# Divisors of the attention rows: inverted in a compact form by way of memory

## The chip, the core and the metric

The kernel runs on one core of a Trainium2 chip. A core has a matrix engine (TensorE: PE in the profile, its weight loads PEld), a vector engine (VectorE, DVE), an engine for activation functions (ScalarE, ACT), a general one (GpSimd, POOL) and one that here only issues transfers (SyncE, SP). Each works through its own instructions in order and waits on semaphores for the others; 16 DMA engines move data between memory (HBM) and the on-chip memory (SBUF). Matmuls write their results into PSUM. The metric is the device time in microseconds. Before the change its median is 1020.46 us over 6 runs (1018.83 to 1021.18).

## The reference

Attention among tokens of one cluster, and then a feed-forward block on the result. q, k and v are 4 x 8 x 768 x 64, with 16 centroids per head:

```python
q_assign = np.argmax(np.einsum('bhsd,hcd->bhsc', q_n, c_n), axis=-1)
k_assign = np.argmax(np.einsum('bhsd,hcd->bhsc', k_n, c_n), axis=-1)
mask = q_assign[:, :, :, None] == k_assign[:, :, None, :]
scores = scale * np.matmul(q, k.transpose(0, 1, 3, 2))
scores = np.where(mask, scores, -1000000000.0)
scores = scores - np.max(scores, axis=-1, keepdims=True)
attn = np.exp(scores)
attn = attn / (np.sum(attn, axis=-1, keepdims=True) + 1e-09)
attn_out = np.matmul(attn, v)
# (B,H,S,D) -> x of (B*S, H*D) = 3072 x 512
h = x @ w_in                    # 512 x 2048
out = (h - np.tanh(h)) @ w_out  # 2048 x 512
```

The weights arrive as 64-bit floats and are turned into 32-bit ones on the chip. What the change touches is the division by `np.sum(attn)`: one number for each query and head.

## The kernel before

Two heads make a pair: 4 batches of 4 pairs, 16 pairs `n`. The 64 feature rows of the first head lie on partitions 0 to 63 and those of the second on 64 to 127. The 768 queries of a pair are worked in two halves of 384, and the 768 keys of a half in three steps of 256: 96 steps in all. In batch 0 the first halves of its four pairs come first and then the second halves; in later batches both halves of a pair follow each other.

A step, in the loop from line 943 on, does this. `begin` (L410) makes the scores of the next step on TensorE and their exponentials on ACT. `select` (L442) masks them on VectorE by comparing the cluster code of each query (`row`, the codes of all queries on every partition, read from memory by a broadcast, L376) with that of the key; POOL adds the masked tiles up (L459, L463). `value` (L465) multiplies them with v. In the first halves of batch 0 (`summed`) the sums are made on TensorE instead (L481), and for pairs 1 to 3 the mask is added to the scores by a matmul with one-hot codes (`hot`, L385 to L398, L429). After the third step of a half `take` (L488) copies the result to `xT`, and `total` (L493) sums the exponentials over the partitions with a matmul against ones. Since that matmul has 64 equal columns per head, its result `den` (128 x 384) holds on each of the 64 partitions of a head the same 384 sums. ACT copies it with the 1e-9 added (L504), and POOL adds it into `wholes` (L505). In the next step `divide` (L507) is called three times: it inverts 128 of the 384 columns each time on VectorE (L510), and the last call multiplies `xT` by the inverse (L513) and has POOL add the inverse into `inverses` (L514). At the end `wholes` and `inverses` are compared with bounds (L1029); they decide with other tests whether a general path must run, which it doesn't for these inputs.

The feed-forward block of a batch is worked beside the attention of the next one, as a list of small items (`plain_items` for batch 0, `strassen_items` with seven products in place of eight for the others); the share of a step in this list is fixed by `fills`. Results wait in PSUM tiles of the pool `ps_f`, which has three. `todo` holds the other work of a step (maskings, routing, the divisions, weight pieces, combining of factors, repeated reads of the inputs) and is spread between the items by `between` (L1007). So the order on each engine is written out by the program, and nothing is moved at run time. In the first 19 steps, two per step at most, the weights arrive in 32 pieces: a POOL transfer of 512 KB (`fetch`, L192; three buffers), one ACT instruction (L139) and three on VectorE (L144, L148, L151). The transfer for the third piece ahead is issued once L148 has freed the buffer.

SP issues in order: loads of q, k and v (L289), the codes out to memory and back (`publish` L369, `spread` L376, `spread_both` L385), the combined weight factors out (L590, L609) and back as `stream` tiles of about 1 MB, asked two ahead (L648), and repeated reads of inputs (L869, L871). At each wait all that stands behind it waits too.

Of the kernel before, what the change touches and what calls it, by code (L numbers as in the profile page):

```python
# [30 lines left out]
F32 = mybir.dt.float32  # L31
# [3 lines left out]
ALU = mybir.AluOpType  # L35
# [3 lines left out]
P = 128  # L39
# [9 lines left out]
MOST_INVERSE = 2.0**5  # L49
SUM_MOST = 2.0**80  # L50
# [7 lines left out]
def kernel(  # L58
# [10 lines left out]
    nc = tc.nc  # L69
# [3 lines left out]
    B, H, S, D = q.shape  # L73
# [4 lines left out]
    HP = H // 2  # L78
# [3 lines left out]
    TB = S // 2  # L82
    HCH = NCH // 2
# [8 lines left out]
    const = ctx.enter_context(tc.tile_pool(name="const", bufs=1))  # L92
    dram = ctx.enter_context(tc.tile_pool(name="dram", bufs=6, space=DRAM))
# [6 lines left out]
    inverses = const.tile([P, TB], F32, name="inverses")  # L100
    wholes = const.tile([P, TB], F32, name="wholes")
    smallest = const.tile([P, 2 * len_pieces], F32, name="smallest")
    largest = const.tile([P, 4 * (HP - 1)], F32, name="largest")
    flag = const.tile([1, 1], I32, name="flag")

    out_r = out.rearrange("(b p j) m -> b j p m", p=P, j=NCH)
# [46 lines left out]
    def fast():  # L153
# [121 lines left out]
        pairs = [(b, p) for b in range(B) for p in range(HP)]  # L275
# [73 lines left out]
        def summed(n: int, half: int):  # L349

            return n < HP and half == 0
# [50 lines left out]
        xT, scores, weights, sums, avs = {}, {}, {}, {}, {}  # L402
# [83 lines left out]
        dens = {}  # L486

        def take(n: int, half: int):  # L488
            if half == 0:
                xT[n] = xp.tile([P, 2, TB], F32, name="xT")  # L490
            nc.scalar.copy(out=xT[n][:, half], in_=avs.pop((n, half)))

        def total(n: int, half: int):  # L493

            s = sums.pop((n, half))
            ps = s
            if not summed(n, half):
                ps = ps_f.tile([P, TB], F32, name="den", tag="f")
                for h in range(2):
                    nc.tensor.matmul(  # L500
                        ps[h * D : h * D + D], lhsT=ones, rhs=s[:, h], start=True, stop=True
                    )
            t = dens[n, half] = sump.tile([P, TB], F32, name="den")
            nc.scalar.activation(out=t, in_=ps, func=ACT.Copy, bias=EPS)  # L504
            nc.gpsimd.tensor_tensor(out=wholes, in0=wholes, in1=t, op=ALU.add)  # L505

        def divide(n: int, half: int, part: int):  # L507
            c = slice(part * P, (part + 1) * P)
            t = dens[n, half]
            nc.vector.reciprocal(out=t[:, c], in_=t[:, c])  # L510
            if part == HCH - 1:
                x = xT[n][:, half]
                nc.vector.tensor_tensor(out=x, in0=x, in1=t, op=ALU.mult)  # L513
                nc.gpsimd.tensor_tensor(out=inverses, in0=inverses, in1=dens.pop((n, half)), op=ALU.add)  # L514
# [68 lines left out]
        def up_maker(q: int):  # L583

            lo, hi = w_in[q], w_in[q + NQ4 // 2]
            a11, a12, a21, a22 = lo[:, 0:CH], lo[:, CH:CD], hi[:, 0:CH], hi[:, CH:CD]

            def keep(which, t):
                for c in range(CH):
                    nc.sync.dma_start(  # L590
                        up_factors[
                            q * FQ : (q + 1) * FQ, :, c, SLOT[which]
                        ].rearrange("i p f -> p i f"),
                        t[:, c].rearrange("p (i f) -> p i f", f=P),
                    )

            return maker(
                (a11, a12, a22), (1, 2, 4),
                ((5, a21, a22, ALU.add), (7, a11, a21, ALU.subtract), (6, 5, a11, ALU.subtract),
                 (3, a12, 6, ALU.subtract)),  # L600
                keep, [P, CH, FQ * P],
            )
# [253 lines left out]
        for n in range(1, HP):  # L856
            b, p = pairs[n]
# [80 lines left out]


        paces = {3: 1, 4: 1}  # L940
        late, divides, makers = [], [], []
        fill, whole, spent, since, over = [], 0.0, 0.0, 0, 1
        for at, (n, half, s) in enumerate(steps):
            b, p = pairs[n]
# [9 lines left out]
            if at == 2 * HALF:  # L954
                makers = [it for i in range(2) for it in up_maker(i)]
# [17 lines left out]
            value(n, half, s)  # L973
            if s == NS - 1:
                take(n, half)
                divides = [lambda n=n, half=half, i=i: divide(n, half, i) for i in range(HCH)]

                if p == HP - 1 and (half == 1 or b == 0):
                    total(n, half)
                    late += divides  # L980
                    divides = []
                if half == 1:
                    load(n + (HP if n < 2 else 2), (2,) if n < 2 or n >= HP else ())

            todo = []
            if following:
                todo += [lambda i=i: select(*following[:2], 2 * following[2] + i) for i in range(2)]
            todo += [stages[i] for i in (5, 3, 4, 2) if i in stages]
            todo += late
            late = []  # L990
            if divides:
                todo.append(lambda n=n, half=half: total(n, half))
                late, divides = divides, []
# [34 lines left out]
        for t, bound in ((inverses, MOST_INVERSE), (wholes, SUM_MOST), (largest, LARGE)):  # L1028
            nc.vector.tensor_scalar(out=t, in0=t, scalar1=bound, scalar2=None, op0=ALU.is_le)  # L1029
        nc.vector.tensor_tensor(out=wholes, in0=wholes, in1=inverses, op=ALU.mult)  # L1030
        checks = [largest]
        if words == 2:
            nc.vector.tensor_scalar(
                out=smallest, in0=smallest, scalar1=HIGH_LEAST, scalar2=None, op0=ALU.is_ge
# [198 lines left out]
```

## Time and profile before

| | us |
|---|---|
| median of 6 runs | 1020.46 |
| profiled execution, its own time | 1023.01 |
| span of that execution, first to last instruction | 1021.2 |
| PE busy | 992.6 (97%) |
| VectorE busy | 613.5 (60%) |
| POOL busy | 552.5 (54%) |
| ACT busy | 298.4 (29%) |
| reciprocals L510, 96 of 128 x 128 | 83.3 |
| POOL adds L505 and L514, 32 each | 35.2 and 41.8 |

In the profile an instruction has its line, engine, operation, the tile written and those read, and its shape as partitions x elements. "Idle before" is the time in which its engine stood idle just before it, with the instruction or transfer that ended most of that. The stages in time are: up to 105 us the first halves of batch 0, to 230 us its second halves, to 403 us batch 1, to 640 us batch 2 and to 866 us batch 3; then only the feed-forward block of batch 3 is left. A transfer issued by SP shows the time of its issue, not of its landing; the landing is read from whoever waits for it, or from the DMA engines' share.

### The profile page before, as it was taken

To read this page: it belongs to the slowest core of one execution; us is meant where nothing else is said; L and a number is where in the kernel's file an instruction comes from. 1 tells how busy PE (TensorE), PEld (TensorE's weight loads), DVE (VectorE), ACT (ScalarE), POOL (GpSimd) and SP (SyncE) were. 2 spreads that over 40 slices of the span, in tenths; PEclk is the share of its full clock that TensorE was granted. 3 is DMA by queue.
4 is the path that set the end of the run, shared out by engine and by line. 5 is a ranking of instruction groups with operands and counts; after the bars stand their busy time and mean duration, and the time that the engine had idled before them with its cause. 6 is when DMAs were issued, how large, how long until landed. Compare 5 with 4: busy or idle time off the path is not lost.

```text
span 1021.2 us, 16368 instructions
## 1 busy us (share of the span) xinstructions
PE 992.6 (97%) x6444; PEld 471.5 (46%) x6444; DVE 613.5 (60%) x1088; ACT 298.4 (29%) x458; POOL 552.5 (54%) x387
## 2 busy tenths in 40 slices
PE   8988899999999999999999999999999999999997
PEld 4433343334444333444455555444445555444664
DVE  6588788336976856676756456766765545543011
ACT  4444334123433233323332222333332211122000
POOL 1124353445655655677789345576879545466600
PEclk9999999999999999999999999999999999999999
DMA  8653423022826633335444555444332322333221
GB/s 214 167 173 127 147 83 116 11 57 74 218 59 178 230 111 100 118 127 173 146 144 140 158 168 152 149 153 138 118 132 91 103 94 66 111 109 121 103 95 38
DMA packets 105736, 127.92 MB, mean 125 GB/s; under 512 B 55604, under 2 KB 85428, under 8 KB 102964
## 3 DMA queue, kind: packets, MB, share of 16 engines
q1 hardware_dynamic: 99268, 105.26, 33.2%
q0 software_dynamic: 6240, 21.50, 6.1%
q8 instruction: 53, 0.87, 0.4%
q14 instruction: 31, 0.25, 0.1%
q10 hardware_dynamic: 144, 0.03, 0.0%
HBM read 105.74 MB, written 21.03 MB: 124 GB/s over the span
## 4 chain that ended last, share of the span: by engine, by line
PE 90%; DVE 4%; ACT 1%; POOL 1%; DMA 1%; issue 1%; ACTq 0%; DVEq 0%; POOLq 0%
PE pu L722 21%; PE pd L770 20%; PE sc L418 13%; PE av L472 13%; PE o L548 8%; PE h L532 7%; PE sim L318 2%; PE den L500 2%; PE pt L299 2%; DMA raw<-in_moe_w_out_dram 1%; PE den L481 1%; PE warm L269 1%; DVE den L510 1%; PE pr L331 1%; ACT t L306 1%
## 5 line engine op out<-in xcount | busy, mean ns | idle before, releaser
L463 POOL TENSOR_TENSOR sum<-sum,e 128x768 f32<-128x768 f32 x112 | 208.6, 1863 | 78.0 <-DVE e L450 74.0
L450 DVE SCALAR_TENSOR_TENSOR e<-row,code,sc 128x384 f32<-128x384 bf16 x336 | 185.9, 607 | 81.6 <-ACT sc L440 70.0
L770 PE MATMUL pd<-stream,G 128*64 128x256 f32 x1728 | 192.4, 380 | 2.4 <-POOL G L713 2.4
L440 ACT ACTIVATE sc<-sc 128x768 f32<-128x768 f32 x168 | 126.0, 793 | 212.1 <-PE sc L418 187.9
L418 PE MATMUL sc<-t,t 64*128 64x384 f32 x768 | 151.7, 513 | 4.8 <-ACT rest L139 2.9
L770 PEld LDWEIGHTS pd<-stream,G 128*64 128x64 f32 x1728 | 123.3, 137 | 70.8 <-issue 8.0
L472 PE MATMUL av<-e,vals 128*64 128x384 f32 x768 | 146.8, 501 | 1.4 <-DVE e L450 0.9
L713 POOL TENSOR_TENSOR G<-G,th 128x768 f32<-128x768 f32 x48 | 86.8, 1820 | 88.7 <-ACT th L712 88.7
L722 PE MATMUL pu<-xT,stream 128*64 128x384 f32 x768 | 134.5, 487 | 0.0
L722 PE MATMUL pu<-diff,stream 128*64 128x384 f32 x576 | 103.5, 488 | 1.0 <-DVE u L708 0.6
L418 PEld LDWEIGHTS sc<-t,t 64*128 64x128 f32 x768 | 66.4, 187 | 79.6 <-issue 39.2
L532 PE MATMUL h<-xT,w_in 128*64 128x384 f32 x512 | 88.9, 498 | 3.8 <-DVE g L539 3.1
L510 DVE RECIPROCAL den<-den 128x128 f32<-128x128 f32 x96 | 83.3, 911 | 11.9 <-POOL wholes L505 11.9
L472 PEld LDWEIGHTS av<-e,vals 128*64 128x64 f32 x768 | 47.1, 136 | 86.9 <-issue 82.6
L548 PE MATMUL o<-w_out,g 128*64 128x512 f32 x384 | 85.9, 593 | 0.0
L722 PEld LDWEIGHTS pu<-xT,stream 128*64 128x64 f32 x768 | 54.6, 137 | 67.3 <-issue 61.8
L459 POOL TENSOR_TENSOR sum<-e 128x768 f32<-128x768 f32 x28 | 56.7, 2025 | 49.3 <-DVE e L450 49.3
L712 ACT ACTIVATE th<-G 128x768 f32<-128x768 f32 x48 | 40.3, 844 | 114.8 <-DVE G L708 114.8
L722 PEld LDWEIGHTS pu<-diff,stream 128*64 128x64 f32 x576 | 40.5, 137 | 51.6 <-issue 44.2
L505 POOL TENSOR_TENSOR wholes<-wholes,den 128x384 f32<-128x384 f32 x32 | 35.2, 1100 | 51.3 <-ACT den L504 51.3
L532 PEld LDWEIGHTS h<-xT,w_in 128*64 128x64 f32 x512 | 37.1, 140 | 51.4 <-issue 45.4
L514 POOL TENSOR_TENSOR inverses<-inverses,den 128x384 f32<-128x384 f32 x32 | 41.8, 1305 | 34.2 <-DVE den L510 34.0
(116 smaller groups left out, 888.6 us busy)
## 6 DMA issues: line engine op xcount, KB each, us to landing
stream<-up_factors SPq DMA_DIRECT2D x24, 896.0 KB
stream<-down_factors SPq DMA_DIRECT2D x21, 1024.0 KB
raw<-in_moe_w_in_dram POOLq DMA_DIRECT2D x16, 512.0 KB, 4.5
raw<-in_moe_w_out_dram POOLq DMA_DIRECT2D x16, 512.0 KB, 4.3
again<-in_moe_w_in_dram SPq DMA_DIRECT2D x32, 256.0 KB
again<-in_moe_w_out_dram SPq DMA_DIRECT2D x32, 256.0 KB
x<-in_q_dram SPq DMA_DIRECT2D x32, 192.0 KB
x<-in_k_dram SPq DMA_DIRECT2D x32, 192.0 KB
```

What stands on the lines that cost most here:

```text
L418: nc.tensor.matmul(sc[i][:, h, 0:TB], lhsT=turned[n, 1][r].rearrange("p a n -> p (a n)")[:, j * P : (j + 1) * P], rhs=turned[n, 0][r, half ...
L440: nc.scalar.activation(out=out, in_=sc[i][:, :, 0:TB], func=ACT.Exp, scale=SCALE)
L450: nc.vector.scalar_tensor_tensor(out=e[:, h], in0=rows[n, half][:, h], scalar=codes[n][:, 1, j // HCH, h, j % HCH : j % HCH + 1], in1=sc[: ...
L459: nc.gpsimd.tensor_tensor(out=s, in0=pair[0], in1=pair[1], op=ALU.add)
L463: nc.gpsimd.tensor_tensor(out=s, in0=s, in1=pair[i], op=ALU.add)
L472: nc.tensor.matmul(avs[n, half][h * D : h * D + D], lhsT=vals[n][:, h, j], rhs=e[i][:, h], start=(j == 0), stop=(j == NCH - 1),)
L510: nc.vector.reciprocal(out=t[:, c], in_=t[:, c])
L532: nc.tensor.matmul(h[r], lhsT=w_in[i][:, c, o * P : (o + 1) * P][:, r], rhs=xT[c][:, half], start=(c == 0), stop=(c == CD - 1),)
L548: nc.tensor.matmul(acc[sub][r], lhsT=gs[f % HF][:, f // HF, sub * P : (sub + 1) * P][:, r], rhs=w_out[f // FQ][:, f % FQ], start=(f == seq ...
L713: nc.gpsimd.tensor_tensor(out=g[:, f].rearrange("p a n -> p (a n)"), in0=g[:, f].rearrange("p a n -> p (a n)"), in1=th.rearrange("p a n -> ...
L722: nc.tensor.matmul(ps[r], lhsT=streams[base + i][:, c, k_, r], rhs=right[c], start=(c == 0), stop=(c == CH - 1),)
L770: nc.tensor.matmul(ps[r], lhsT=left(i)[:, r], rhs=t[:, i], start=(i == 0), stop=(i == HF - 1))
```

## The change

For the first three pairs of each batch (24 of the 32 halves) the sums are no longer inverted on 128 partitions. `last(n)` names the fourth pair, which keeps the old way. For the others four stages are called in four successive steps, the first in the step in which `total` stood before:

- `total`: as before up to the copy L504; then, in place of the POOL add, two SP transfers write one row of 384 sums of each head to memory (`list`).
- `compact`: an SP transfer reads the 768 sums back as 128 partitions x 6 into a place of its own in the new tile `each`.
- `invert`: VectorE inverts the 128 x 6; an SP transfer writes them to memory (`back`), and two more read each head's row of 384 onto its 64 partitions of `den`.
- `scale`: VectorE multiplies `xT` by `den`.

The POOL adds into `wholes` and `inverses` remain for the fourth pairs alone. At the end three VectorE instructions of 128 x 144 compare `each` with the bounds.

```diff
+    each = const.tile([P, 2 * B * (HP - 1), 2 * TB // P], F32, name="each")
...
             nc.scalar.activation(out=t, in_=ps, func=ACT.Copy, bias=EPS)
-            nc.gpsimd.tensor_tensor(out=wholes, in0=wholes, in1=t, op=ALU.add)
+            if last(n):
+                nc.gpsimd.tensor_tensor(out=wholes, in0=wholes, in1=t, op=ALU.add)
+                return
+            lists[n, half] = dram.tile([2, TB], F32, name="list")
+            for h in range(2):
+                nc.sync.dma_start(lists[n, half][h : h + 1], t[h * D : h * D + 1])
+        lists, spots = {}, {}
+        def last(n: int):
+            return pairs[n][1] == HP - 1
+        def compact(n: int, half: int):
+            spots[n, half] = each[:, len(spots)]
+            nc.sync.dma_start(
+                spots[n, half], lists.pop((n, half)).rearrange("h n -> (h n)").rearrange("(p i) -> p i", p=P)
+            )
+        def invert(n: int, half: int):
+            t = spots[n, half]
+            nc.vector.reciprocal(out=t, in_=t)
+            back = dram.tile([2, TB], F32, name="back")
+            nc.sync.dma_start(back.rearrange("h n -> (h n)").rearrange("(p i) -> p i", p=P), t)
+            for h in range(2):
+                nc.sync.dma_start(
+                    dens[n, half][h * D : h * D + D], back[h : h + 1].to_broadcast([D, TB])
+                )
+        def scale(n: int, half: int):
+            x = xT[n][:, half]
+            nc.vector.tensor_tensor(out=x, in0=x, in1=dens.pop((n, half)), op=ALU.mult)
...
-        late, divides, makers = [], [], []
+        late, divides, makers, later = [], [], [], {}
...
-                divides = [lambda n=n, half=half, i=i: divide(n, half, i) for i in range(HCH)]
+                if last(n):
+                    divides = [lambda n=n, half=half, i=i: divide(n, half, i) for i in range(HCH)]
+                else:
+                    for i, stage in enumerate((total, compact, invert, scale)):
+                        later.setdefault(at + i, []).append(
+                            lambda stage=stage, n=n, half=half: stage(n, half)
+                        )
...
-            todo += late
+            todo += late + later.pop(at, [])
...
-        checks = [largest]
+        inverse = each.rearrange("p a b -> p (a b)")
+        fits = inverses[:, 0 : inverse.shape[1]]
+        nc.vector.tensor_scalar(
+            out=fits, in0=inverse, scalar1=MOST_INVERSE, scalar2=None, op0=ALU.is_le
+        )
+        nc.vector.scalar_tensor_tensor(
+            out=fits, in0=inverse, scalar=1.0 / SUM_MOST, in1=fits, op0=ALU.is_ge, op1=ALU.mult
+        )
+        checks = [fits, largest]
```

## The prediction, made before the changed kernel was run

> **What bounds the kernel now.** I read the page first, then the busy time by stage, then TensorE's own waits, then the chain of waits and the order of time where TensorE waits.
>
> The page and the busy time by stage (columns: length, then PE, PEld, DVE, ACT, POOL busy with instruction counts, granted clock, DMA share, GB/s):
> ```profile
> span 1021.2 us, 16368 instructions
> PE 992.6 (97%) x6444; PEld 471.5 (46%) x6444; DVE 613.5 (60%) x1088; ACT 298.4 (29%) x458; POOL 552.5 (54%) x387
> L510 DVE RECIPROCAL den<-den 128x128 f32<-128x128 f32 x96 | 83.3, 911 | 11.9 <-POOL wholes L505 11.9
> ...
> 60.00:130.00 70.00, 58.63 (x322) 23.67 (x318) 58.04 (x89) 28.31 (x47) 27.96 (x29) 0.92 0.48 156
> 130.00:405.00 275.00, 273.37 (x1502) 109.72 (x1500) 188.88 (x282) 93.88 (x147) 145.94 (x92) 1.00 0.37 111
> 405.00:875.00 470.00, 467.15 (x3246) 233.28 (x3242) 291.39 (x546) 131.59 (x198) 310.83 (x211) 1.00 0.41 133
> ```
> TensorE is the bound, and a full one: from 130 to 875 us it idles 1.63 + 2.85 = 4.5 us of 745. VectorE's 83.3 us of reciprocals are mostly beside it. Only in 60 to 130 us does TensorE idle (11.4 us), and there VectorE is busy 58 of 70 us. TensorE's waits in that stage, in 130 to 865 us, and the chain:
> ```profile
> PE h L532 <- DVE g L539: 3.1, 1, 3.1
> PE sc L418 <- ACT rest L139: 2.9, 1, 2.9
> PE sc L429 <- DVE hot L397: 2.5, 1, 2.5
> ...
> PE sim L318 <- ACT t L306: 1.2, 5, 0.2
> PE pd L770 <- POOL G L713: 0.9, 2, 0.5
> ...
> 61.46 2.50 DVE den L510 x3
> 78.76 2.59 DVE den L510 x3
> 86.25 4.37 DMA raw<-in_moe_w_out_dram
> 95.62 2.59 DVE den L510 x3
> ```
> The chain runs through three sets of reciprocals. Those at 61.46 (pair 1) and 78.76 (pair 2) go away; the one at 95.62 is pair 3, the last of its batch, and stays. The 2.5 us wait at 67.3 to 69.8 us is for the one-hot rows that stand on VectorE behind the first set. The 2.9 us wait, 88.6 to 91.5, ends with the masking at 90.23, which follows weight pieces behind the second set.
>
> **What goes.** 24 of the 32 halves lose three reciprocals (72 x 0.911 = 65.6 us of VectorE), the POOL add into `wholes` (1.0 to 1.1) and that into `inverses` (1.3): 24 x 2.4 = 58 us of POOL. The x multiply (0.56) stays, two steps later. From 130 us on the cover is TensorE's own work, so 21 of the halves are worth nothing by themselves. Pair 0's set (40.6 to 43.2 us) lies where TensorE is 97 to 100% busy: nothing either.
>
> **What comes.** Per half six SP transfers in place of none: two rows out (list), one spread in (compact), one out (back), two broadcasts; 144 in all. VectorE gets one 128x6 reciprocal. No row has that shape: the 128x1 one takes 0.16 us, a 128x128 one 0.91; by count I take 0.16 + 0.04 = 0.2. ACT and PE keep their instructions. List and compact have a step or more and nobody waits for them. Back and broadcast have one step: VectorE inverts at step +2 and multiplies at +3, in order, so a late broadcast holds maskings, evictions and weight pieces behind it. SP stands at three waits per half (sum copied, list landed, back landed), and behind it queue code rows, stream loads and repeated weight reads. Code rows have a step to spare. Streams are asked two ahead, each for 9 us of matmuls (7 products of 1.29 us): the 2 to 6 us that SP stands are covered; without that, each us is a us of TensorE.
>
> **The two hops.** Nearest rows:
> ```profile
> 39.54 0.32 SPq L369 DMA_DIRECT2D q_codes<-qc  x1
> ...
> 40.87 1.27 SPq L385 DMA_DIRECT2D hot<-q_codes  x2
> ...
> 46.94 0.42 DVE L393 TENSOR_SCALAR hot<-hot,mine_code 128x768 bf16<-128x768 bf16 x1 [0.44 <-DMA hot<-q_codes]
> ```
> A small write to DRAM lets SP go on 40.87 - 39.54 = 1.33 us after its issue (2.69 at 57.10, with weight loads about). The broadcast: code rows of 192 KB, as much as ours, issued at 204.46, kept the DMA engines busy to 207.1, 2.6 us. The hot broadcast, twice our bytes with loads behind it, took 6.1 us. So the chain from reciprocal to usable divisor is 1.3 + 2.6 + 0.1 = 4.0 us at best, and 2.7 + 6.1 = 8.8 us loaded at worst; I take 4.6 to 5.4 in the weight stage, nearer the rows of our size. The steps there are 4.6 us of TensorE, in batch 1 some 7.2 us (24 steps in 229 to 402.7), later 9.7 (46 in 402.7 to 847).
>
> (The Trainium skill, "DMA: Bandwidth & Descriptors", section "Anatomy of one DMA", gives about 2.0 us fixed per transfer plus bytes over 436 GB/s. By it two hops are an estimated 4.5 us. Its Specifications say that pieces under 512 B pay a read-modify-write, and ours are 24 B: a rule against this change, and no row here has 24 B pieces. The 256 B pieces of the code write came back in 1.33 us.)
>
> **The sum in 40 to 130 us**, along VectorE:
> - Pair 0: inverted at 54.4 (after the routing of pair 3). VectorE reaches the multiply at 57.1; the divisor is there at 54.6 + 4.6 = 59.2. Cost 2.1 + 0.56 = 2.7 us (bounds: 1.5 + 0.56 to 6.3 + 0.56).
> - Pair 1: the set at 61.37 goes, 2.57 + 0.56, and so does the stretch of the piece behind it (L144 took 1.23 us beside POOL's `inverses` add at 64.09, else 0.42): gain 3.9. The one-hot rows come 3.9 - 2.7 = 1.2 us earlier, and TensorE's 2.5 us wait shrinks to 1.3. Then its inversion 0.2, two weight pieces (2 x 1.9 us) and the multiply: wait 5.4 - 3.8 = 1.6, with the multiply 0.56: 2.4 us back.
> - Pair 2: the set at 78.76 goes with VectorE's 0.90 us wait for POOL's `wholes`: 0.90 + 2.58 + 0.56, and 0.8 of stretch: 4.8, less 0.2. Running shift 1.2 - 2.4 + 4.6 = 3.4 us at the masking of 90.23, less than the 2.5 + 2.9 us of TensorE's two waits, so TensorE can follow.
> - Pair 2's multiply now stands behind pair 3's at 98.8: +0.56. After that the same chain of weight pieces runs on (the 3.1 us wait at 123.6 stays). Net -2.8.
>
> Clock: after the 2.5 us wait eight den matmuls took 2.56 us by the chain, elsewhere 1.29; after the 2.9 us wait the eight scores 2.55, elsewhere 1.49. After the 1.66 us wait at 107.37 the granted clock stayed 1.00. With the first wait at 1.3 us its 1.3 us return to TensorE, but VectorE sets the end there; I take 0.5 of gain, between 0 and 2.3.
> (The skill, "TensorE: Matmul & The Clock Gate", section "What's actually happening", halves the clock after an idle window of about 3.4 us. By it neither wait should have cost clock and this term is 0; the rows show the loss after 2.5 us.)
>
> **Elsewhere.** POOL freed: the two 0.47 us waits for G (524, 760 us) stand behind a POOL that is 90% busy: -0.3 (0 to 0.9). At the end three more VectorE instructions of 128x144 (two bounds, one product) stand before the add at 873.85 that TensorE awaits (0.60 us at 874.45). By the 128x64 and 128x384 rows (0.19 and 0.35; 0.22 and 0.56): 0.2 + 0.3 + 0.25 = +0.75. For late multiplies after 130 us I take +0.1. Sum: -2.8 - 0.5 - 0.3 + 0.75 + 0.1 = -2.75 us on the profiled execution's 1023.01 us (span 1021.2). That one stands 0.25% above the median of the runs shown, 1020.46; from the median, **1017.7 us**.
>
> **Rivals.**
> - *Full relief*: divisors come in 4.0 us, both waits go (5.4) and the clock with them (2.3), less 0.56 and 0.75: -6.4, at most -8: 1012.5 to 1014. For it: VectorE alone leads to both waits. Against: the weight loads (ACT waits for raw loads at nearly every piece in 60 to 91 us) take 3.6 to 4.5 us each and a piece needs one per 2.2 us with three buffers.
> - *Eaten*: by the terms above each us on the chain costs 2 us, one at pair 0 and one at pair 1; without the clock term the sum is zero at a chain of 6.2 us and within 2 us of zero from 5.2 to 7.2. At 6.5: pair 0 costs 4.0 + 0.56, pair 1 2.7 + 0.76, the shift is 3.9 - 4.6 - 3.5 + 4.6 = 0.4, and with 0.56 + 0.75 + 0.1 - 0.3 the end is 0.7 us later: 1021.2. For it: the write of 2.69 us at 57.10 and DMA engines at a share of 0.78 in 60 to 70 us, so that 2.7 + 3.8 is near. Against: pair 0's chain falls into 54 to 59 us, where the share is 0.16.
> - *Slower*: the same multiply, with a chain beyond 7.2 us, since the 24 B pieces or the raw weight loads of 512 KB slow both hops; VectorE holds the one-hot rows and the weight pieces behind the multiply, and TensorE waits longer at 67 us than now. At the loaded bound of 8.8 us: pair 0 6.3 + 0.56, pair 1 5.0 + 0.76, shift 3.9 - 6.9 - 5.8 + 4.6 = -4.2, end 4.2 + 1.1 = 5.3 us later: 1025.8. For it: the hot broadcast's 6.1 us. Against: it had 768 B pieces, 512 of them, and 768 KB of loads around it.
>
> The later halves are costed at 0.1: their cover is the step plus TensorE's three result buffers (7.2 + 2.6 us in batch 1, 9.7 + 2.6 later, at 1.29 us a product and two buffers ahead). Beyond that each us of the chain costs one per half, 6 and 12 times. Batch 1's factor writes stand in the same queue, but in its inversion steps SP's order has them after the broadcasts, and the DMA share there is 0.4.
>
> **Chances.** My case 0.38 (own range 1014 to 1018.4), full relief 0.12, eaten 0.26, slower 0.24. About 0.2% (2 us) is what a measurement here can tell from no change. Faster 0.50, same 0.26, slower 0.24. Range: 1012.5 (full relief's bound) to 1024.0 (a chain of 8 us), which leaves out the worse half of the slower case and little else.
>
> **What would show it.** Right: no reciprocals of 128x128 outside pair 3; VectorE idle 1 to 3 us before the multiply near 57 and 72 us, released by the broadcast; TensorE's waits at 67 and 88 us shortened; 130 to 865 us as full as now. Wrong: VectorE's wait for the broadcast in the hundreds of us, new TensorE waits behind L450, L539 or L708 after 130 us, or stream loads landing late behind SP.

## The result and the profile after

The changed kernel takes 1023.37 us (median of 18 runs, 1021.29 to 1024.26), the kernel before 1021.09 us (38 runs, 1018.35 to 1023.62). The ratio is 1.0022, 95% interval 1.0015 to 1.0029: 2.3 us slower, where 2.75 us faster was forecast. The profiled execution of the changed kernel took 1022.54 us (span 1020.7), 0.8 us under its median; that of the kernel before stood 1.9 us above its own. So a stage that looks 2 us shorter in the one profile than in the other says nothing yet, and the readings below rest on waits inside one profile and on the measured ratios.

The page of the kernel after:

```profile
span 1020.7 us, 16553 instructions
PE 992.1 (97%) x6444; PEld 472.2 (46%) x6444; DVE 545.0 (53%) x1043; ACT 298.3 (29%) x458; POOL 490.8 (48%) x339
```

Its busy time by stage (columns as for the kernel before):

```profile
60.00:130.00 70.00, 59.41 (x326) 24.28 (x324) 53.11 (x89) 29.22 (x48) 23.14 (x26) 0.93 0.51 161
130.00:405.00 275.00, 274.06 (x1514) 110.30 (x1512) 165.13 (x268) 94.35 (x148) 118.22 (x76) 1.00 0.42 121
405.00:875.00 470.00, 465.54 (x3232) 232.54 (x3230) 258.43 (x522) 130.68 (x197) 285.71 (x187) 1.00 0.43 137
```

VectorE lost 68.5 us of work and POOL 61.7 us; TensorE's busy time is what it was, and from 130 to 865 us it is as full as before (731.5 us of 735 in both). So the place to look is again the weight stage, and after it the end. There VectorE now waits for something that did not exist before. Its queue there (start, duration, instruction, and in brackets the idle time before it with what ended that):

```profile
54.81 0.18 DVE L528 RECIPROCAL each<-each 128x6 f32<-128x6 f32 x1
...
61.81 0.56 DVE L538 TENSOR_TENSOR xT<-xT,den 128x384 f32<-128x384 f32 x1 [4.21 <-DMA den<-back]
...
69.85 0.48 DVE L394 TENSOR_SCALAR hot<-hot,mine_code 128x768 bf16<-128x768 bf16 x1
...
70.48 0.18 DVE L528 RECIPROCAL each<-each 128x6 f32<-128x6 f32 x1
...
80.21 0.56 DVE L538 TENSOR_TENSOR xT<-xT,den 128x384 f32<-128x384 f32 x1 [5.53 <-DMA den<-back]
```

The divisors of pair 0 land 6.7 us after their inversion (54.99 to 61.72 us), those of pair 1 9.5 us after (70.66 to 80.12). VectorE stands 4.2 and 5.5 us at the two multiplies, with weight pieces and the one-hot rows behind it. The chain of waits (start, duration, what) has the hops where the reciprocals stood:

```profile
55.02 1.41 DMA back<-each
...
56.98 4.74 DMA den<-back
...
63.98 3.74 DMA raw<-in_moe_w_in_dram
67.80 0.68 ACT rest L140
68.48 0.71 ACT e L441
...
69.85 0.48 DVE hot L394
70.69 4.26 DMA back<-each
...
75.49 4.63 DMA den<-back
```

SP's queue shows the two halves of a hop, and that the broadcasts now stand ahead of the query codes:

```profile
55.02 0.35 SPq L530 DMA_DIRECT2D back<-each  x1
56.45 1.13 SPq L532 DMA_DIRECT2D den<-back  x2
57.68 0.50 SPq L370 DMA_DIRECT2D q_codes<-qc  x1
61.74 1.26 SPq L386 DMA_DIRECT2D hot<-q_codes  x2
```

The write `back` lets SP go on 56.45 - 55.02 = 1.43 us after its issue, but 74.96 - 70.69 = 4.27 us for pair 1 and 4.78 us for pair 2, when raw weight loads are under way. The code write behind the broadcasts takes 61.74 - 57.68 = 4.06 us; before, it took 2.69.

TensorE's waits of the kernel after in 40 to 140 us, where before had 3.1 + 2.9 + 2.5 us at the top:

```profile
PE sc L419 <- ACT e L441: 5.1, 2, 2.9
PE h L565 <- DVE xT L538: 3.1, 1, 3.1
PE av L473 <- ACT xT L492: 1.1, 1, 1.1
```

So the waits did not go; they changed names. How VectorE's wait becomes TensorE's is in the chain above and in these two lines, the first of POOL, which issues the weight loads, the second of TensorE:

```profile
63.98 0.74 POOL L193 DMA_DIRECT2D raw<-in_moe_w_in_dram  x1 [6.87 <-DVE w_in L149]
...
69.23 2.93 PE L419 MATMUL sc<-t,t 64*128 64x384 f32 x8 [2.85 <-ACT e L441]
```

While VectorE stands at pair 0's multiply it frees no weight buffer, so POOL issues no load for 6.87 us. ACT's weight instruction waits for the load (67.80), ACT's exponentials stand behind it in order (68.48), and TensorE waits 2.85 us for them, where it waited 2.5 us for the one-hot rows before. At pair 1's multiply POOL's pause is 7.46 us, and TensorE's wait behind it, again for exponentials on ACT, is 2.30 us (87.93).

### The profile page after: what moved, and what is told of

Same layout as the page of the kernel before. It is cut to its first block, busy times and chain, and to the rows that moved or that the text cites. A ratio compares the mean times of both kernels' runs of the same rounds, so it can differ in the third digit from the quotient of the medians.

```text
span 1020.7 us, 16553 instructions
## 1 busy us (share of the span) xinstructions
PE 992.1 (97%) x6444; PEld 472.2 (46%) x6444; DVE 545.0 (53%) x1043; ACT 298.3 (29%) x458; POOL 490.8 (48%) x339
## 4 chain that ended last, share of the span: by engine, by line
PE 87%; DVE 5%; DMA 3%; ACT 2%; issue 1%; POOL 1%; SPq 0%; ACTq 0%; DVEq 0%; POOLq 0%
PE pd L803 20%; PE pu L755 20%; PE sc L419 13%; PE av L473 12%; PE o L581 8%; PE h L565 6%; PE sim L319 2%; PE den L501 2%; PE pt L300 2%; DMA raw<-in_moe_w_out_dram 1%; DMA den<-back 1%; DMA raw<-in_moe_w_in_dram 1%; PE warm L270 1%; ACT t L307 1%; POOL G L746 1%
## 5 line engine op out<-in xcount | busy, mean ns | idle before, releaser
L464 POOL TENSOR_TENSOR sum<-sum,e 128x768 f32<-128x768 f32 x112 | 205.4, 1834 | 129.2 <-DVE e L451 119.6
L755 PE MATMUL pu<-xT,stream 128*64 128x384 f32 x768 | 134.6, 487 | 0.7 <-DVE top L340 0.7
L755 PE MATMUL pu<-diff,stream 128*64 128x384 f32 x576 | 103.5, 488 | 1.9 <-DVE u L741 1.6
L755 PEld LDWEIGHTS pu<-xT,stream 128*64 128x64 f32 x768 | 54.6, 137 | 68.4 <-issue 61.1
L755 PEld LDWEIGHTS pu<-diff,stream 128*64 128x64 f32 x576 | 40.6, 137 | 52.5 <-issue 44.3
L741 DVE TENSOR_TENSOR G<-pu,u 128x384 f32<-128x384 f32 x72 | 39.7, 552 | 40.6 <-PE pu L755 40.5
L814 DVE TENSOR_TENSOR c<-pd,du 128x256 f32<-128x256 f32 x36 | 15.2, 421 | 69.1 <-PE pd L803 69.1
L581 PEld LDWEIGHTS o<-w_out,g 128*64 128x64 f32 x384 | 27.5, 137 | 50.6 <-issue 50.6
```

The costliest lines, as they stand in the source:

```text
L464: nc.gpsimd.tensor_tensor(out=s, in0=s, in1=pair[i], op=ALU.add)
L581: nc.tensor.matmul(acc[sub][r], lhsT=gs[f % HF][:, f // HF, sub * P : (sub + 1) * P][:, r], rhs=w_out[f // FQ][:, f % FQ], start=(f == seq ...
L755: nc.tensor.matmul(ps[r], lhsT=streams[base + i][:, c, k_, r], rhs=right[c], start=(c == 0), stop=(c == CH - 1),)
```

## The experiments

Each ratio is that of a kernel's runs to runs of the kernel before on the same chip, with its 95% interval. The first theory (W) was that the loss arises in the weight stage, where the hops eat the relief; the rival (L) that the later halves, their transfers and the longer end cost it.

**The two ways split by batch.** In the first kernel batch 0 keeps the old division, in the second only batch 0 has the compact one.

```diff
 def last(n: int):
-    return pairs[n][1] == HP - 1
+    return n < HP or pairs[n][1] == HP - 1     # first kernel
+    return n >= HP - 1                         # second kernel
```

> The changed kernel with batch 0 on the old path; batches 1 to 3 (18 halves) keep the compact way and the end its three added VectorE instructions. Theory W (the loss comes from the first halves of batch 0, where the chain from reciprocal to divisor took 6.7, 9.5 and 10.3 us in the profile of the changed kernel): the time returns to that of the kernel before plus at most the 0.75 us of the end, ratio 1.000 to 1.0008. Theory L (the loss comes from the later halves, their transfers and the end): still 1.5 to 2.5 us slower, ratio 1.0015 to 1.0025.

> The opposite: the compact way in batch 0 alone (6 halves). Theory W: the whole loss, 1.5 to 2.5 us, ratio 1.0015 to 1.0025. Theory L: ratio at most 1.0008.

Measured: 1.0011 (1.0000 to 1.0022) and 1.0007 (0.9995 to 1.0018). Their losses add up to 1.0018, near the 1.0022 of the whole change, although the end's three instructions stand in both kernels. Neither theory has the loss alone. How it is shared the intervals leave open; the second kernel's includes no loss at all. The division of batch 0 is not the gain that it was forecast to be.

**The transfers taken away, or only not waited for.** In the first of these kernels none of the six transfers is issued; 24 halves are multiplied by their sums and so left undivided. In the second all are issued and the inversion still waits for the compact sums, but the multiply by the sums stands beside the inversion, so that VectorE waits for no broadcast (24 halves undivided again). The edit of the second:

```diff
 def invert(n: int, half: int):
     t = spots[n, half]
     nc.vector.reciprocal(out=t, in_=t)
+    x = xT[n][:, half]
+    nc.vector.tensor_tensor(out=x, in0=x, in1=dens[n, half], op=ALU.mult)
     back = dram.tile([2, TB], F32, name="back")
...
 def scale(n: int, half: int):
-    x = xT[n][:, half]
-    nc.vector.tensor_tensor(out=x, in0=x, in1=dens.pop((n, half)), op=ALU.mult)
+    dens.pop((n, half))
```

> The changed kernel without any of its 144 transfers: VectorE inverts a tile of ones and multiplies x by the sums themselves (the 24 halves are left undivided), so that the freed VectorE and POOL time is there and no hop. Theory W: the forecast's relief without its price: TensorE's two waits at 67 and 88 us shrink to nearly nothing, 3 to 6 us faster than before, ratio 0.994 to 0.997. Theory L: the relief is worth nothing on TensorE's path: ratio 0.9995 to 1.0008.

> The changed kernel with all its transfers, but x is multiplied by the sums (the 24 halves are left undivided) right after the small reciprocal, ahead of the transfer back: the transfers run and SP stands at its waits, but VectorE waits for none of the broadcasts. Theory W, with VectorE's wait for the broadcast as the mechanism: within 1 us of the kernel without hops, ratio 0.995 to 0.998. If instead the transfers by themselves cost the time (DMA engines, SP standing): near the changed kernel, ratio 1.001 to 1.0025.

Measured: 0.9956 (0.9941 to 0.9971) without transfers, 0.9998 (0.9988 to 1.0008) with them. So there is a relief, worth 4.4 us, and with the transfers it is gone even where nobody waits for the broadcasts. That the rows are left undivided is not by itself the gain, since they are so in both kernels. In that kernel's profile VectorE stands 5.1 us in the weight stage at the inversion, for the compact sums:

```profile
DVE each L528 <- DMA each<-list: 5.1, 2, 3.3
...
DVE hot L394 <- DMA hot<-q_codes: 3.0, 1, 3.0
```

**The multiply two steps later.** The changed kernel, with more of VectorE's own work between inversion and multiply in the first halves of pairs 0 and 1.

```diff
+    stretch = 2 if n < 2 and half == 0 else 0
     for i, stage in enumerate((total, compact, invert, scale)):
+        i += stretch * (i == 3)
         later.setdefault(at + i, []).append(
```

> The changed kernel, but in batch 0's first halves of pairs 0 and 1 the multiply stands five steps after the sums in place of three, so that VectorE has two more steps of its own work between the inversion and the wait for the broadcast. If the loss in the weight stage is VectorE standing at the multiply (it stood 4.2 and 5.5 us there in the profile of the changed kernel): both waits fall under 1 us, and the ratio to the kernel before is 0.998 to 1.000, 2 to 4 us under the changed kernel's 1.0022. If it is the transfers themselves, which share the DMA engines with the weight loads, the ratio stays at 1.001 to 1.002.

Measured: 0.9990 (0.9979 to 1.0000), 3.3 us under the changed kernel. Both waits at the multiply are gone from the profile. This is what VectorE's standing at the broadcasts costs. But it brings the kernel back to where it was before and little further.

**The compact way for a part of the first halves.** Pairs 0 and 1 alone, with the late multiply; the same with the comparisons at the end moved behind six more items of the last feed-forward block; pair 2 alone, with the multiply where the change has it; and pairs 0, 1 and 2, with the late multiply for 0 and 1. All other halves are divided in the old way (`last` becomes a test of pair and half; each line with + is one kernel's).

```diff
-    return pairs[n][1] == HP - 1
+    return n >= 2 or half == 1      # pairs 0 and 1
+    return n != 2 or half == 1      # pair 2
+    return n >= 3 or half == 1      # pairs 0, 1 and 2
...
+for it in tail[2:8]:                # the second kernel: ahead of the comparisons
+    it[2](lambda: None)
...
-for it in tail[2:16]:
+for it in tail[8:16]:
```

> The compact way only for the first halves of pairs 0 and 1 of batch 0, with the multiply five steps after the sums; the other 30 halves are divided as before. If the relief of VectorE in the weight stage is worth what the kernel without transfers showed there (about 6 us) and the hops eat only part of it when nobody stands at the broadcast: ratio 0.9965 to 0.9985, and nothing of the loss of about 0.5 us each near 480 and 715 us, since the order of the later steps is the old one. If the hops eat the relief by loading the DMA engines beside the weights: ratio about 1.000.

> As the kernel with only two compact halves, and the comparisons with the bounds at the end stand on VectorE behind six more items of the last feed-forward block. If TensorE's wait of 0.6 us at 874 us (1.6 in the changed kernel) comes from these comparisons standing ahead of the factor's add, it goes: 0.5 to 1.0 us under the kernel with two compact halves, ratio 0.996 to 0.998. If the wait only moves to a later factor: no difference from that kernel.

> The compact way for one half alone, the first half of pair 2 in batch 0; the other 31 are divided as before. Pair 2's three reciprocals with their wait for POOL and the stretched weight piece behind them (4.8 us on VectorE by the prediction's sum) go, and nothing is added beside pairs 0 and 1. If it is this relief that the changed kernel lives on: the masking that stood at 90.2 us comes 3 to 4.5 us earlier, the score step 13 that began at 91.5 us 2 to 3 us, and the ratio is 0.9965 to 0.998. If the raw weight loads set the time there whatever VectorE does: no change, 0.999 to 1.0005.

> The compact way only for the first halves of pairs 0, 1 and 2 of batch 0, the multiply of pairs 0 and 1 five steps after the sums; all later halves as before, with their old order of items. This is the kernel with the late multiplies (0.9990) without the later halves. If these cost it 0.5 us each near 480 and 715 us through the routing's place, and 0.5 at the end: 1 to 1.7 us under it, ratio 0.9970 to 0.9985. If the later halves cost nothing: 0.9985 to 0.9995.

Measured: 1.0065 (1.0051 to 1.0079), 1.0080 (1.0064 to 1.0096), 0.9995 (0.9984 to 1.0006) and 1.0001 (0.9988 to 1.0013). None brought the gain that was expected; for pair 2 alone the ratio is that of the other case (0.999 to 1.0005). The kernel with pairs 0, 1 and 2 is the one with the late multiply without its later halves, and it is not faster than that one (0.9990): in this pairing the later halves cost nothing that can be seen. Pairs 0 and 1 alone lose 6.9 us. VectorE's queue of that kernel shows where a part of it is:

```profile
64.42 0.69 DVE L152 CUSTOM_DVE_ANT_0 w_in<-w_in,rest 128x1024 uint16<-128x1024 uint16 x1
69.29 0.42 DVE L394 TENSOR_SCALAR hot<-hot,mine_code 128x768 bf16<-128x768 bf16 x1 [4.18 <-DMA hot<-q_codes]
...
80.64 2.58 DVE L543 RECIPROCAL den<-den 128x128 f32<-128x128 f32 x3 [0.91 <-POOL wholes L507]
```

Where pair 1's reciprocals stood VectorE now waits for the one-hot rows, which are a transfer that it cannot hasten: their operation starts at 69.29 us, against 69.05 before. Then pair 2's set, which stays in this kernel, starts 1.9 us later than before (78.76). What goes is time in which VectorE would have waited anyway. The rest of the 6.9 us (some 2 us between 104 and 132 us, and 2 us in the last stage) is not explained by what I ran. Moving the comparisons made a new wait instead of removing one: beside a POOL instruction of 1.9 us two of them took 2.00 and 1.78 us, where they had taken 0.35 and 0.17, and TensorE waited 3.4 us for a factor behind them. Pair 2 alone brought the score step 13 forward by 2.5 us in its profile (91.51 to 88.97), as expected; of that, 0.5 us is left in the ratio, inside the interval.

**The order of the later steps.** As the kernel with batch 0 on the old way, but inversion and multiply ride on items that stood in the list already, and empty items take the place of those left out.

```diff
-        later.setdefault(at + i, []).append(
+        (later if i < 2 else joined).setdefault(at + i, []).append(
...
+    later[at + 1] += [lambda: None] * 2
...
+if at in joined:
+    todo[-1:] = [lambda fs=[todo[-1], *joined.pop(at)]: [f() for f in fs]]
```

> Batch 0 is divided the old way and batches 1 to 3 in the compact way, with the inversion and the multiply tied to items that stood in the list anyway and empty items in place of those left out, so that the number of items per step, and with it the place of the routing, is that of the kernel before. If the loss of about 0.5 us each near 480 and 715 us is the routing that moved to another place between the feed-forward items: TensorE's waits for the routing there fall back to what they were before, and the ratio is at most 1.0008, from the 0.7 us of the three instructions at the end. If the transfers cost it, both losses remain and the ratio is 1.001 to 1.002, as in the kernel that only keeps batch 0 on the old way.

Measured: 1.0009 (1.0001 to 1.0018), as against 1.0011 without the edit. In the profile TensorE's waits for the routing's `top` (L340, 0.7 us in two near 480 and 715 us, which all kernels with compact later halves have and the kernel before has not) are gone. So the place of the routing did cause them, since the transfers are all still there; but 0.7 us is too little to be seen in the times. What remains is the end, where the wait at L755 is 1.5 us against 0.6 before.

**The broadcasts behind the query codes.** The kernel with pairs 0, 1 and 2, and the changed kernel with the late multiply, each with pair 0's broadcasts issued one step later.

```diff
+    backs[n, half] = back
+    if n or half:
+        spread_back(n, half)
...
+if n == 0 and half == 0:
+    later.setdefault(at + 3, []).append(lambda: spread_back(0, 0))
```

> As the kernel with three compact halves, but the two broadcasts of pair 0's divisors are issued one step later, behind the write of the query codes and their broadcasts. If those broadcasts in front of it are what made the code write take 4.1 to 4.6 us in place of 2.7 and the one-hot rows land after 69 us: the code write is back at 2.7 to 3.0 us, the one-hot rows land at 68 to 69 us, TensorE's wait for them falls to 2 us or less, and the ratio is 0.9960 to 0.9980, 0.5 to 1.5 us under the kernel that issues them at once. If the write is slow for the weight loads alone, it stays at 4 us and there is no difference.

> The changed kernel with two edits in batch 0's first halves: the multiply of pairs 0 and 1 five steps after the sums, and the broadcasts of pair 0's divisors one step later, behind the query codes. By the order of the queue: code write 2.7 to 3.0 us, one-hot rows earlier than in the kernel with the late multiply alone (69.9 us there), ratio 0.9975 to 0.9990. If the order of these transfers doesn't matter: 0.9990 as without the second edit.

Measured: 1.0004 (0.9995 to 1.0013) and 1.0000 (0.9991 to 1.0009). The mechanism was there and the gain was not: the code write is back at 59.99 - 56.99 = 3.00 and 2.72 us, TensorE's wait for the one-hot rows falls to 2.2 and 2.1 us, and its clock is not cut behind it. Then another wait takes the place. VectorE's queue of the first of the two:

```profile
68.76 0.42 DVE L394 TENSOR_SCALAR hot<-hot,mine_code 128x768 bf16<-128x768 bf16 x1 [4.21 <-DMA hot<-q_codes]
69.09 0.31 DVE L398 TENSOR_SCALAR hot<-hot,mine_code 128x384 bf16<-128x384 bf16 x1
69.43 0.56 DVE L544 TENSOR_TENSOR xT<-xT,den 128x384 f32<-128x384 f32 x1
71.82 0.19 DVE L528 RECIPROCAL each<-each 128x6 f32<-128x6 f32 x1 [1.84 <-DMA each<-list]
```

And ACT's queue of the same kernel:

```profile
78.66 0.67 ACT L140 ACTIVATE rest<-raw 128x512 uint32<-128x512 uint32 x1 [4.07 <-DMA raw<-in_moe_w_in_dram]
79.23 0.46 ACT L492 COPY xT<-av 128x384 f32<-128x384 f32 x1
```

VectorE stands for the one-hot rows, and right behind them for pair 1's compact sums. From 65 to 71.9 us it works on no weight piece, so no buffer comes free and POOL, whose queue this is, issues no load:

```profile
64.26 0.53 POOL L193 DMA_DIRECT2D raw<-in_moe_w_in_dram  x1 [1.16 <-ACT e L441]
73.59 0.74 POOL L193 DMA_DIRECT2D raw<-in_moe_w_in_dram  x1 [8.80 <-DVE w_in L149]
```

That load lands at 78.6 us; ACT has stood at it for 4.07 us, ACT's copy of the attention result stands behind it in order, and TensorE waits 5.2 us for that copy at `av`. This execution is the slowest of its kernel's (1024.26 us, median 1020.74), but the second kernel's, which took its median, shows the same: POOL pauses 8.65 us and TensorE waits 5.5 us at `av`. A wait of VectorE's for a small transfer has become a late weight load, and this a wait of TensorE's.

**What eats the relief: the transfers, or those who wait for them?** Three kernels tell it apart: all transfers issued while VectorE waits for none, because it inverts a tile of ones that goes to memory and back (24 halves multiplied by sums beside the inversion, undivided); no transfers in the three first halves alone (those three halves undivided; its edit is that of the kernel without transfers, for these halves); and the true compact way with the inversion of pairs 0 and 1 one step later.

```diff
+    spare = const.tile([P, 2 * B * (HP - 1), 2 * TB // P], F32, name="spare")   # ones
...
-            t = spots[n, half]
+            t = spare[:, len(dens_done)]
+            dens_done.append(n)
             nc.vector.reciprocal(out=t, in_=t)
```

```diff
-    later.setdefault(at + i, []).append(
+    later.setdefault(at + i + (n < 2) * (0, 0, 1, 2)[i], []).append(    # late inversion
```

> All transfers run, but VectorE waits for none: it inverts a tile of ones of its own, which is what goes to memory and back, and multiplies by the sums, so the rows stay undivided (24 halves). Beside it stand the kernel without transfers (0.9956) and the one in which VectorE waits only for the compact sums at the inversion (0.9998). If those waits at the inversion (5.1 us in the weight stage) are what eats the relief: 0.9955 to 0.9975. If it is the transfers' load on the queue and the DMA engines: 0.9985 to 1.0000.

> No transfers, and only in the first halves of pairs 0, 1 and 2 of batch 0 (these three halves multiplied by sums and left undivided, a small reciprocal of ones in place of the three large ones); the other 29 are divided as before. If the whole relief lies in the weight stage and the later halves only cost (1.1 us by the routing's place, and most of 0.7 at the end): 1 to 2 us under the kernel without any transfers, ratio 0.9940 to 0.9955. If some of the relief lies later: 0.996 to 0.998.

> The compact way for the first halves of pairs 0, 1 and 2 of batch 0; pairs 0 and 1 are inverted one step later than in the kernel with three compact halves (1.0001), the multiply stays five steps after the sums. If VectorE's wait for the compact sums is what eats the relief: its 2.1 us there go and the ratio is 0.9970 to 0.9990. If it is the transfers' load: no change, 0.9995 to 1.0005.

The first run of the kernel that waits for nothing said nothing: its bounds were tested on sums that nobody had inverted, so the general path ran (4860 us). With the bounds tested on the inverted tile:

> All transfers run, but VectorE waits for none: it inverts a tile of ones of its own, which goes to memory and back and is tested at the end, and multiplies by the sums, so the rows stay undivided (24 halves). Beside it stand the kernel without transfers (0.9956) and the one in which VectorE waits only for the compact sums at the inversion (0.9998). If those waits at the inversion are what eats the relief: 0.9955 to 0.9975. If it is the transfers' load on the queue and the DMA engines: 0.9985 to 1.0000.

Measured: 0.9960 (0.9947 to 0.9972), with every transfer on the queues. That is the 0.9956 of the kernel without any, within the intervals, which are some 1.3 us to each side. The transfers themselves cost nothing that these runs can tell; waiting for them does. The relief in the three first halves alone gave 0.9963 (0.9950 to 0.9976), the same within the intervals, so it lies in the weight stage; that the later halves would then cost another 1 to 2 us was not borne out. The later inversion ran at 1.0035 (1.0023 to 1.0048), against both of its cases: it took no wait away. VectorE's waits of that kernel in 50 to 140 us:

```profile
DVE xT L538 <- DMA den<-back: 3.6, 2, 3.0
DVE each L528 <- DMA each<-list: 3.2, 1, 3.2
```

The later `back` now stands behind the one-hot broadcasts, and 67.90 - 61.19 = 6.71 us pass between its issue and that of the broadcast behind it.

**The place of the work in place of its amount.** The kernel before, with no compact half and no new transfer: pair 1's multiply and POOL add stand behind the one-hot rows, and pair 2's three reciprocals with what follows stand behind the masking of 90.2 us, in the 3.2 us that VectorE waited for POOL's sum of pair 3.

```diff
-            if part == HCH - 1:
+            if part == HCH - 1 and (n, half) != (1, 0):
+                finish(n, half)
+
+        def finish(n: int, half: int):
...
-                    late += divides
-                    divides = []
+                    late += held + divides
+                    divides, held = [], []
...
-            late = []
+            late = [lambda: finish(1, 0)] if at == 2 * NS else []
...
+                if (n, half) == (2, 0):
+                    held, divides = divides, []
```

> The kernel before, without compact halves or new transfers, and two moves in batch 0's first halves: pair 1's multiply and its POOL add stand behind the one-hot rows of 69 us, and pair 2's three reciprocals, multiply and add stand behind the masking of 90.2 us, where VectorE waited 3.2 us for POOL's sum of pair 3. If what the changed kernel could win is the place of VectorE's work, and not its amount: the one-hot rows' operation starts at 68.0 to 68.7 us, TensorE's wait there is 2.2 us or less and its clock is not cut (the score step 10 begins 1.5 to 2 us earlier), the masking comes 2 to 4 us earlier, and the ratio is 0.9955 to 0.9985. If the weight loads set the pace there in any order: 0.9990 to 1.0010.

Measured: 0.9973 (0.9963 to 0.9983), 1017.81 us against 1020.56: it beats both kernels, with 96 large reciprocals and all of POOL's additions still in it. VectorE's queue of this kernel:

```profile
66.80 1.57 DVE L393 TENSOR_SCALAR hot<-hot,mine_code 128x768 bf16<-128x768 bf16 x1
...
86.78 2.18 DVE L450 SCALAR_TENSOR_TENSOR e<-row,code,sc 128x384 f32<-128x384 bf16 x4
88.88 2.57 DVE L510 RECIPROCAL den<-den 128x128 f32<-128x128 f32 x3
91.48 0.83 DVE L516 TENSOR_TENSOR xT<-xT,den 128x384 f32<-128x384 f32 x1
92.24 2.56 DVE L510 RECIPROCAL den<-den 128x128 f32<-128x128 f32 x3
```

The masking comes 3.4 us earlier than at 90.23 (this execution began 0.8 us ahead), and pair 2's set fills the gap without a wait in front of pair 3's. One part of the expectation missed: the one-hot rows were ready earlier than I had taken (the operation starts at 66.80, without a wait), TensorE's wait there fell to 2.1 us, and yet its clock was cut behind it.

## Why the prediction was wrong

The ratios of four kernels tell it best, each as measured above:

| kernel | ratio | step from the line above |
|---|---|---|
| no transfers (undivided) | 0.9956 | |
| transfers, VectorE waits for none (undivided) | 0.9960 | +0.0004 |
| VectorE waits for the compact sums alone (undivided) | 0.9998 | +0.0038 |
| the change: it waits for the broadcasts too | 1.0022 | +0.0024 |

In the third line the write `back` also hangs on the compact sums, so SP's queue is held by that link too; the 0.0038 are for both.

- **The bound and what goes: right.** TensorE bounds; VectorE lost 68.5 us, POOL 61.7, and from 130 to 865 us nothing follows from it. The 128x6 reciprocal takes 0.18 us (0.2 taken).
- **The two hops: the step that failed.** The chain from reciprocal to divisor was taken as 4.6 to 5.4 us, "nearer the rows of our size", with 8.8 as the loaded worst. In the first halves it is 6.73, 9.46 and 10.25 us. The broadcast was undersized in all three, 5.2 to 5.4 us (2.6 plus a little taken); the write was right for pair 0, 1.43 us, and undersized for the others, 4.27 and 4.78 (1.3 to 2.7 taken). VectorE stood at the multiplies for the difference, and with the multiplies moved two steps later that loss went (1.0022 to 0.9990). The argument that pair 0's chain falls into a stretch with a DMA share of 0.16 rests on a misreading: in the busy time of the kernel before, shown below this list, 0.16 is the mean of 50 to 60 us, of which 54 to 57 us has 0.00 and 57 to 60, into which the broadcast runs, 0.54. The broadcast took 5.27 us. The nearest row by load, the hot broadcast's 6.1 us, was the better one. In the quietest later step, at 774 us, the chain does take 4.2 us (write 1.42).
- **The sum with the measured chains.** Pair 0's wait is 4.21 us and not 2.1, pair 1's 5.53 and not 1.6. By the prediction's own sum the shift is 3.9 - (4.21 + 0.56) - (5.53 + 0.76) + 4.6 = -2.6 at the masking, and with 1.1 for the rest the end is 3.7 us later. Measured: 2.3. So the sum has the right sign with the measured chains, but not the right parts: of the 3.7 us it puts 2.6 + 0.56 = 3.2 into the weight stage, where the kernel with batch 0 alone loses 0.7 us (-0.5 to 1.8), its end included.
- **The way to TensorE: another than the sum's.** The rival that came true is the slower one, at about its point (a chain beyond 7.2 us); TensorE's wait near 67 us is longer, as it said, 2.85 us against 2.48. But the way was another: the sum follows VectorE to the one-hot rows and has no term for the weight loads, whose issue paused 6.87 and 7.46 us behind VectorE's waits, while ACT's exponentials stood behind its weight instructions. That the measured time lies inside the stated range says little: the range held the slower rival too.
- **"List and compact ... nobody waits for them": wrong as soon as the broadcasts are out of the way.** In the changed kernel VectorE comes late to the inversion and the wait is hidden. Where it comes in time it stands 5.1 us there, and by the ratios this is the larger of the two costs in the table.
- **"Code rows have a step to spare": wrong in this stage.** The code write went from 2.69 to 4.06 us behind the broadcasts. Put back in order it fell to 2.7 to 3.0, without a gain in time.
- **Pair 1's gain of 3.9 us: too large.** It counts VectorE's work before the one-hot rows as time won. Without pair 1's reciprocals, in the kernels without transfers or with the broadcasts behind the codes, VectorE still waits 3.3 to 4.2 us for their transfer, and TensorE's 2.5 us become 1.9 to 2.2, not 1.3 (2.4 in the kernel that waits for none of the new transfers). In two others (the wait for the compact sums alone, and the later inversion) it was 1.2 and 1.1, and the gain was lost at once to the 4.8 and 5.1 us that TensorE then waited at `av` for ACT's copy.
- **Clock: no gain.** The granted clock in 60 to 130 us is 0.93 after 0.92; behind the 2.85 us wait it is 0.50 in 70 to 72 us.
- **POOL's G waits: nothing** (2.4 us before, 2.3 after; 0.3 taken). **The end: right in kind**, TensorE's wait there grew from 0.6 to 1.6 us, 1.0 where 0.75 was taken. **Late multiplies: right.** VectorE stands 26.3 us in 11 places at the multiply, 16.6 of them after 130 us, and TensorE is as full there as before up to 865 us. Not in the sum: the routing's new place, 0.7 us of TensorE's waits.

The busy time of the kernel before around pair 0's chain (the last but one number of a line is the DMA share):

```profile
50.00:60.00 10.00, 10.00 (x64) 4.45 (x62) 6.97 (x13) 5.86 (x11) 2.18 (x3) 1.00 0.16 54
54.00:57.00 3.00, 3.00 (x19) 1.26 (x17) 2.31 (x5) 2.52 (x5) 0.53 (x1) 1.00 0.00 0
57.00:60.00 3.00, 3.00 (x22) 1.36 (x20) 2.80 (x6) 2.28 (x5) 1.65 (x2) 1.00 0.54 177
```

What stays open: why the kernels with pairs 0 and 1 alone and with the later inversion lose 7 and 4 us, more than their waits in the weight stage show; and how much of the loss belongs to the later halves (1.1 us, 0 to 2.2, in the kernel that has only them; nothing seen when they are taken from the kernel with the late multiply).

## What to carry to other kernels

Work taken from an engine in a stage of in-order queues is worth only what the next arrival lets through: ask what lands last there, and price a wait in the queue (4 to 5 us here) against the work it replaces (2.6 us). The round trip through memory here had to be priced by the transfers that run beside it, not by the rows of its own size, and the wait for it by every queue that stands behind the waiting engine: VectorE's held the weight loads, they held ACT, and ACT held TensorE. Here putting the old work into a gap of the same engine won 2.7 us, with no transfer at all.

## What the runs showed of the hardware

- A 3 KB write to memory in 24-byte pieces let its queue go on after 1.4 to 1.6 us in 15 of the 24 cases of the changed kernel, after 1.7 to 3.0 us in seven, and after 4.3 and 4.8 us beside 512 KB weight loads (6.7 us in the kernel with the later inversion). Its 24-byte pieces show no cost of their own at its quickest (1.40 us, against 1.33 us for the code write's 256-byte pieces). The Trainium skill ("DMA: Bandwidth & Descriptors", section "Anatomy of one DMA — SWDGE (gpsimd) path") gives about 2.0 us fixed per transfer, for transfers that GpSimd issues; the ones here are SP's, so the estimate of 4.5 us for two hops applies the figure to another path. The quick write is below 2.0 us, and the chains of pairs 1 and 2 took twice those 4.5 us.
- All 144 transfers together cost nothing measurable where VectorE waits for none of them (0.9960 against 0.9956, each known to some 0.0013).
- TensorE's clock after a wait of some 2 us went either way: no cut after 2.13, 2.14 and 2.23 us (eight den matmuls at 1.46 us), a cut after 2.10, 2.40 and 2.48 us (2.1 to 2.8 us for the same eight). After the 2.10 us wait the granted clock in 70 to 72 us was 0.50, after the 2.13 us wait 1.00. The skill ("TensorE: Matmul & The Clock Gate", section "What's actually happening") speaks of an idle window of about 3.4 us; in these runs shorter waits cut the clock.
- VectorE instructions stretched beside POOL's work on tiles in on-chip memory: the 128x384 comparison took 2.00 us against 0.35, the one-hot operation 1.57 against 0.42.
